# Linear attention feeding a gated FFN on one core: tiles turned by DMA, later loads, full-width transposes of q, a reordered beginning

## Chip, cores, metric

One core of one Trainium2 chip. The metric is device time in microseconds (us) of one execution; lower is better. The kernel before takes 325.9 us (median of 3 runs, 325.85 to 326.36).

In the profiles PE is TensorE (PEld its weight loads), DVE is VectorE, ACT is ScalarE, POOL is GpSimd and SP is SyncE; L503 is line 503 of that run's kernel.py, and x4 at the end of a line means four instructions in a row. Lines beginning with two numbers give start and length in us.

## The reference, cut to what matters

```
pos = arange(S);  theta = pi/2 * pos / S
phi(x) = concat(relu(x) * cos(theta), relu(x) * sin(theta))       # q, k: 8 batches x 8 heads x 576 x 64
kv  = einsum('bhsf,bhsd->bhfd', phi(k), v);   z = sum_s phi(k)
x   = (phi(q) @ kv) / (phi(q) @ z + 1e-6)                         # 4608 tokens x 512
out = (silu(x @ w_gate) * (x @ w_val)) @ w_out                    # 512 -> 1536 -> 512
```

The kernel works in 9 groups of 512 tokens, each of four tiles of 128. For a group it computes x of each tile, turns it (tokens by features becomes features by tokens), runs 12 blocks of gate and value products with silu and product between them, then the output stage: four tiles of 12 accumulating products. Batches are counted from 0 in the code, so its batch 1 is the "batch two", and its batch 2 the "batch three", of the change's name.

## The kernel before: the parts that the change touches

The program fixes the order of each engine's instructions, so this change is largely one of order. `at("b9", ...)` hangs work behind the second half of block 9, `at((1, 2), ...)` behind a part of the output stage. In the list of words each word is one step: G1.0 is the gate product of block 1 for token tile 0.

```python
def qturn_pe(b, j, lo, hi, eng):                   # q of batches 0 (last slot) and 1
    ps = take(1).bitcast(BF16).rearrange("p (c x) -> p c x", x=P)
    for c in range(lo, hi):
        for i in range(2):                         # two half-width transposes of the raw q
            nc.tensor.transpose(out=ps[i * D:(i + 1) * D, c - lo], in_=raws[b, "q"][:, 2 * j + i, c],
                                identity=ident)
    relu_op(eng, qt_of(b)[...], ps[...])           # relu while PSUM is emptied

def x_turn(t, fast=False):
    if fast:                                       # 4 PE transposes and an ACT copy
        x_turn_pe(t)
        x_turned(t, "act")
    else:
        nc.sync.dma_start_transpose(out=xT_of(t), in_=st["x", t])
# ... loads, in the order of issue:
load_slots(1, "q", 0, CUT)
load_wo(0); load_wo(1); load_wo(2)
load_slots(1, "q", CUT, NC)
for nm in ("q", "k", "v"):
    load(2, nm)
# ... group 0: blocks 0-5 by a list of words, blocks 6-11 in halves "a" and "b" of two tiles each
at("b11", q_(1, 0, 0), q_(1, 1, 0), lambda: kv_mm(1), lambda: kv_out(1))
at((1, 0), turn(4, True), a_(6, 0))                # slots of the output stage: tiles 4-7 made and turned
at((1, 2), turn(5, True), a_(7, 0))
at((2, 0), turn(6, True))
at((2, 2), turn(7, True))
```

## Time and profile before

| | kernel before |
|---|---|
| span of the profiled run | 324.6 us |
| first gate product (G1.0) | 16.41 us |
| 28 half-width transposes of q | 39.66 us |
| output stage of group 0 | 41.74 to 55.48 us (13.74) |
| group 1 to the end | 269.1 us |

These are starts in PE's order of instructions. PE is busy 98% of the span. The lines themselves stand in the prediction below.

### The profile page before, as it was taken

How to read it: one execution, taken by the hardware profiler on the slowest of the kernel's cores; microseconds unless marked ns; L12 is line 12 of the kernel's file. 1: busy time of each engine (PE TensorE's matmuls, PEld its weight loads, DVE VectorE, ACT ScalarE, POOL GpSimd, SP SyncE). 2: the span in 40 equal slices, each digit the busy share in tenths (PEclk: the TensorE clock that was granted, in tenths of full speed). 3: DMA queues.
4: the chain of work that ended last, by engine and by line, in shares of the span. 5: the costliest groups of instructions: out<-in, count | busy, mean ns of one | idle time of the engine just before them, and what ended most of it. 6: DMA issues, size and time to landing. Idle time of an engine off the chain costs nothing.

```text
span 324.6 us, 6212 instructions
## 1 busy us (share of the span) xinstructions
PE 318.0 (98%) x2474; PEld 164.6 (51%) x2474; DVE 181.8 (56%) x366; ACT 132.3 (41%) x247; POOL 34.8 (11%) x58
## 2 busy tenths in 40 slices
PE   7999999999999999999999999999999999999995
PEld 3589855454545444544454445444554445444443
DVE  7775866976575647565657555755564236423420
ACT  7553565943653335332642354344432132213311
POOL 6755200002002000110002000200000000000000
PEclk9999999999999999999999999999999999999999
DMA  7999999499676997699689969794921411240014
GB/s 264 215 199 199 205 205 221 70 125 149 147 125 80 185 153 128 93 170 163 120 111 140 164 129 130 119 186 110 134 46 34 106 26 32 44 103 17 2 32 97
DMA packets 71660, 40.37 MB, mean 124 GB/s; under 512 B 47184, under 2 KB 66384, under 8 KB 71632
## 3 DMA queue, kind: packets, MB, share of 16 engines
q1 hardware_dynamic: 49280, 22.29, 37.9%
q0 software_dynamic: 22192, 17.57, 35.5%
q8 instruction: 19, 0.31, 0.4%
q10 hardware_dynamic: 160, 0.13, 0.1%
q14 instruction: 9, 0.07, 0.1%
HBM read 37.75 MB, written 9.44 MB: 145 GB/s over the span
## 4 chain that ended last, share of the span: by engine, by line
PE 95%; DMA 2%; DVE 1%; ACT 0%; SPq 0%; issue 0%; ACTq 0%
PE banks L503 58%; PE banks L539 28%; PE banks L276 3%; PE banks L390 2%; DMA first_q<-in_q_dram 2%; PE banks L475 1%; PE banks L434 1%; PE banks L149 1%; PE banks L558 1%; PE banks L264 0%; PE banks L316 0%; PE banks L372 0%; SPq L117 0%; DVE qwT L360 0%; ACT ob L561 0%; ACT qf L339 0%
## 5 line engine op out<-in xcount | busy, mean ns | idle before, releaser
L514 DVE TENSOR_TENSOR ht<-sg,banks 128x512 bf16<-128x512 bf16 (+2 forms) x122 | 75.8, 625 | 68.1 <-PE banks L503 62.3
L509 ACT ACTIVATE sg<-banks 128x512 bf16<-128x512 f32 (+2 forms) x122 | 66.9, 548 | 113.6 <-PE banks L503 109.0
L503 PE MATMUL banks<-xT,wv_sb 128*128 128x512 bf16 (+2 forms) x488 | 112.8, 355 | 0.1
L503 PE MATMUL banks<-xT,wg_sb 128*128 128x512 bf16 (+2 forms) x488 | 112.6, 355 | 0.0
L539 PE MATMUL banks<-wo_sb,ht 128*128 128x512 bf16 x420 | 94.3, 379 | 0.0
L503 PEld LDWEIGHTS <-wv_sb 128*128 128x128 bf16 x488 | 47.2, 98 | 46.7 <-issue 0.4
L503 PEld LDWEIGHTS <-wg_sb 128*128 128x128 bf16 x488 | 45.7, 98 | 41.6
L539 PEld LDWEIGHTS <-ht 128*128 128x128 bf16 x420 | 40.1, 98 | 45.2 <-issue 0.2
L546 ACT COPY ob<-banks 128x512 f32<-128x512 f32 x18 | 10.5, 585 | 51.2 <-PE banks L539 49.2
L232 DVE TENSOR_TENSOR r_q<-raw_q,tab 128x1152 bf16<-128x1152 bf16 x24 | 17.9, 754 | 20.2 <-ACT raw_q L215 20.2
L546 DVE COPY ob<-banks 128x512 f32<-128x512 f32 x17 | 11.8, 691 | 28.9 <-PE banks L539 28.0
L236 DVE TENSOR_TENSOR v<-raw_v,tab 128x1152 bf16<-128x1152 bf16 x31 | 23.0, 752 | 0.3 <-ACT raw_v L570 0.3
L411 DVE TENSOR_TENSOR x<-banks,rec 128x512 bf16<-128x512 f32 (+1 forms) x32 | 21.5, 674 | 1.1
L714 POOL COPY hold<-phit 1x2 bf16<-1x2 bf16 x5 | 0.9, 176 | 155.1 <-DMA phit<-r_q 155.1
L215 ACT ACTIVATE raw_q<-raw_q 128x576 bf16<-128x576 bf16 x24 | 15.7, 680 | 0.8 <-DMA raw_q<-in_q_dram 0.8
L215 ACT ACTIVATE raw_k<-raw_k 128x576 bf16<-128x576 bf16 x24 | 16.0, 675 | 0.0
L390 PEld LDWEIGHTS <-phit 128*128 128x128 bf16 (+1 forms) x240 | 9.9, 100 | 6.0 <-issue 1.3
L390 PE MATMUL banks<-kv,phit 128*128 128x65 bf16 (+1 forms) x240 | 11.5, 195 | 0.0
L149 PE MATMUL banks<-zeros 128*128 128x64 bf16 (+1 forms) x66 | 8.7, 290 | 1.0 <-DVE zeros L144 1.0
L299 DVE CAST kv<-banks 64x260 bf16<-64x260 f32 x12 | 5.1, 428 | 7.4 <-ACT kv L299 7.4
L276 PEld LDWEIGHTS <-raw_k 64*64 64x64 bf16 x504 | 7.5, 106 | 2.6 <-issue 2.1
L276 PE MATMUL banks<-v,raw_k 64*64 64x130 bf16 x504 | 8.7, 218 | 0.0
(79 smaller groups left out, 134.3 us busy)
## 6 DMA issues: line engine op xcount, KB each, us to landing
out_dram<-ob SPq DMA_DIRECT2D x70, 128.0 KB, 2.4
raw_k<-in_k_dram POOLq DMA_DIRECT2D x7, 576.0 KB, 9.6
raw_q<-in_q_dram POOLq DMA_DIRECT2D x6, 576.0 KB, 6.1
raw_v<-in_v_dram POOLq DMA_DIRECT2D x6, 576.0 KB, 12.3
wo_sb<-in_moe_w_out_dram POOLq DMA_DIRECT2D x3, 512.0 KB, 12.7
wg_sb<-in_moe_w_gate_dram POOLq DMA_DIRECT2D x5, 256.0 KB, 9.0
wv_sb<-in_moe_w_val_dram POOLq DMA_DIRECT2D x5, 256.0 KB, 9.2
wo_sb<-in_v_dram SPq DMA_DIRECT2D x2, 576.0 KB, 4.1
```

Of the source, the lines that this page charges most:

```text
L149: nc.tensor.matmul(out=ps, lhsT=zeros, rhs=zeros[:, 0:cols].unsqueeze(1).to_broadcast([P, 4, cols]), start=True, stop=True)
L215: nc.scalar.activation(out=out, in_=in_, func=AF.Relu)
L232: nc.vector.tensor_tensor(out=st[b, "q"][:, g], in0=o.unsqueeze(2).to_broadcast([P, NC, 2, D]), in1=tab, op=ALU.mult)
L236: nc.vector.tensor_tensor(out=v2s[b % 2][:, g, :, :, 0:D], in0=(first if b == 0 and g == 0 else {"v": raw_of(b, "v")})["v"][:, g].unsqueez ...
L276: nc.tensor.matmul(out=ps[i * D:(i + 1) * D, e, j * 2 * D1:(j + 1) * 2 * D1], lhsT=raws[b, "k"][es, g, c], rhs=v2s[b % 2][es, g, c, :, 0:D ...
L390: nc.tensor.matmul(out=ps[ms, e, g * D1:(g + 1) * D1], lhsT=phit[b][:, e, g, c:c + n].rearrange("p c s -> p (c s)"), rhs=kv2s[b % 2][:, e, ...
L411: nc.vector.tensor_tensor(out=st["x", t].rearrange("p (y e d) -> p e y d", e=2, d=D)[:, :, ys], in0=ps[:, :, 0:2 * J * D1].rearrange("p e ...
L503: nc.tensor.matmul(out=st["f", tg, fc, lo][i], lhsT=(wg_sb, wv_sb)[i][:, kc, fs], rhs=xT[tg][:, ts, kc], start=(kc == 0), stop=(kc == KC - 1))
L509: nc.scalar.activation(out=sg[:, 0:n], in_=st["f", tg, fc, lo][0], func=AF.Silu)
L514: nc.vector.tensor_tensor(out=hts[tg % 2][:, fc, r:r + n], in0=st.pop(("s", tg, fc, lo))[:, 0:n], in1=ps[1], op=ALU.mult)
L539: nc.tensor.matmul(out=o_ps[t], lhsT=hts[tg % 2][:, fc, r:r + P], rhs=wo_sb[:, fc], start=(fc == 0), stop=(fc == FC - 1))
L546: (nc.scalar.copy if t % 2 == 0 else nc.vector.tensor_copy)(out=ob, in_=ps)
```

## The change

Its intent: take transposes off PE (tiles 4 and 5 are turned by DMA), keep the DMA engines free for these turns (k and v of batch three are loaded only when tile 4's turn has landed), use one full transpose for a pair of half ones, use 512 columns instead of 2 x 256 in blocks 6 to 11, and order the beginning better. Full transposes need the two heads of a pair side by side, so relu now runs on DVE ahead of the transposes and writes them so.

```diff
+    def relu_slots(b, lo, hi):
+        ...
+        relu_op("dve", st["qp"][:, b, lo:hi].rearrange("p c j (i d) -> p c (j i) d", i=2),
+                raws[b, "q"][:, :, lo:hi].rearrange("p g c d -> p c g d"))
     def qturn_pe(b, j, lo, hi, eng):
-            for i in range(2):
-                nc.tensor.transpose(out=ps[i * D:(i + 1) * D, c - lo], in_=raws[b, "q"][:, 2 * j + i, c], identity=ident)
-        relu_op(eng, qt_of(b)...
+            nc.tensor.transpose(out=ps[:, c - lo], in_=st["qp"][:, b, c, j], identity=ident)
+        copy_op(eng, qt_of(b)...
-    for nm in ("q", "k", "v"):
-        load(2, nm)
+    load(2, "q")
-    words = """ cq0@act cq1@act tq0 qr0@dve qw0.0 qw0.1 rk1.0@act rk0.0@dve z8 kv0.0 ...
+    words = """ cq1@act cq0@dve tq0 qr0@dve rk0.0@act rk1.0@dve qw0.0 qw0.1 z6 kv0.0 ...
+    at("a8", lambda: relu_slots(0, NC - 1, NC))
-    for g, s in enumerate(("a10", "a11", "b8", "b9")):
+    for g, s in enumerate(("b9", "b9", "b10", "b10")):
         at(s, lambda g=g: vmul(1, g))
+        if g == 2:
+            at(s, lambda: relu_slots(1, 0, CUT))
+    def load_2():
+        nc.gpsimd.tensor_copy(out=hold2, in_=xT[1][0:1, 0, 0, 0:2])
+        for nm in ("k", "v"):
+            load(2, nm)
+    at((0, 1), turn(4), load_2)
-    at((1, 0), turn(4, True), a_(6, 0))
+    at((1, 0), turn(5), a_(6, 0))
-    at((1, 2), turn(5, True), a_(7, 0))
+    at((1, 2), a_(7, 0))
-    for nm, f in order:
-        ffn_fc(0, f, *((HALF, GH) if nm == "b" else (0, HALF)))
+    for f in range(6, FC):
+        ffn_fc(0, f)
-    steps0 = [(piece, t) for piece in range(3) for t in range(2)] + [(piece, t) for t in (2, 3) for piece in range(3)]
+    steps0 = [(piece, t) for piece in range(3) for t in range(3)] + [(piece, 3) for piece in range(3)]
```

Cut: pools one buffer larger, the choice of PSUM banks, den and rec of tile 0 in halves, the rest of the words, and a later use of k and v of batch three in group 1.

More of the change, by code (lines that the diff above doesn't have):

```diff
@@ L50 @@
     phip = ctx.enter_context(tc.tile_pool(name="phip", bufs=2))
-    xp = ctx.enter_context(tc.tile_pool(name="xp", bufs=3))
+    xp = ctx.enter_context(tc.tile_pool(name="xp", bufs=4))
     xtp = ctx.enter_context(tc.tile_pool(name="xtp", bufs=3))
     smp = ctx.enter_context(tc.tile_pool(name="smp", bufs=3))
-    sgp = ctx.enter_context(tc.tile_pool(name="sgp", bufs=4))
+    sgp = ctx.enter_context(tc.tile_pool(name="sgp", bufs=5))
     obp = ctx.enter_context(tc.tile_pool(name="obp", bufs=4))
@@ L66, in take @@
     def take(n, hold=None):
-        free = [b for b in range(0, 8, n) if not any(b <= x < b + n for r in held.values() for x in r)]
-        b0 = min(free, key=lambda b: sorted(used[b:b + n], reverse=True))
+        taken = {x for r in held.values() for x in r}
+        free = [b for b in range(0, 8, n) if not any(b <= x < b + n for x in taken)]
+        b0 = min(free, key=lambda b: (n == 1 and hold is not None and hold[0] == "o" and b ^ 1 not in taken,
+                                      sorted(used[b:b + n], reverse=True)))
         if hold is not None:
@@ L258, in qturn_dma @@
         )
+    def relu_slots(b, lo, hi):
+        if "qp" not in st:
+            both = rel.tile([P, G, NC, 2, D], BF16, name="r_q").rearrange("p g c w d -> p (g c w d)")
+            st["qp"] = both.rearrange("p (b c j x) -> p b c j x", b=2, c=NC, j=J)
+        relu_op("dve", st["qp"][:, b, lo:hi].rearrange("p c j (i d) -> p c (j i) d", i=2),
+                raws[b, "q"][:, :, lo:hi].rearrange("p g c d -> p c g d"))
     def qturn_pe(b, j, lo, hi, eng):
@@ L262, in qturn_pe @@
         for c in range(lo, hi):
-            for i in range(2):
-                nc.tensor.transpose(out=ps[i * D:(i + 1) * D, c - lo], in_=raws[b, "q"][:, 2 * j + i, c],
-                                    identity=ident)
-        relu_op(eng, qt_of(b)[:, :, j, lo:hi].rearrange("p e c s -> p c e s"),
+            nc.tensor.transpose(out=ps[:, c - lo], in_=st["qp"][:, b, c, j], identity=ident)
+        copy_op(eng, qt_of(b)[:, :, j, lo:hi].rearrange("p e c s -> p c e s"),
                 ps[:, 0:hi - lo].rearrange("p c (e s) -> p c e s", e=2))
@@ L395, in a_tile2, with x_den, x_rec @@
         x_of(t, ps)
-    def x_den(t, ps):
-        den = smp.tile([P, H, 1], FP32, name="den")
+    def x_den(t, ps, ys=slice(0, 4)):
+        if ys.start == 0:
+            st["den", t] = smp.tile([P, H, 1], FP32, name="den")
         nc.vector.tensor_single_scalar(
-            out=den.rearrange("p (e y) o -> p e y o", e=2),
-            in_=ps[:, :, 0:2 * J * D1].rearrange("p e (y x) -> p e y x", x=D1)[:, :, :, D:D1], scalar=1e-6, op=ALU.add)
-        st["den", t] = den
-    def x_rec(t):
-        rec = smp.tile([P, H, 1], FP32, name="rec")
-        nc.vector.reciprocal(out=rec, in_=st.pop(("den", t)))
-        st["rec", t] = rec
-        st["x", t] = xp.tile([P, d_model], BF16, name="x")
+            out=st["den", t].rearrange("p (e y) o -> p e y o", e=2)[:, :, ys],
+            in_=ps[:, :, 0:2 * J * D1].rearrange("p e (y x) -> p e y x", x=D1)[:, :, ys, D:D1], scalar=1e-6, op=ALU.add)
+    def x_rec(t, ps, ys=slice(0, 4)):
+        if ys.start == 0:
+            st["rec", t] = smp.tile([P, H, 1], FP32, name="rec")
+            st["x", t] = xp.tile([P, d_model], BF16, name="x")
+        nc.vector.reciprocal(out=st["rec", t].rearrange("p (e y) o -> p e y o", e=2)[:, :, ys],
+                             in_=st["den", t].rearrange("p (e y) o -> p e y o", e=2)[:, :, ys])
     def x_mul(t, ps, ys=slice(0, 4)):
@@ L418, in x_of @@
         x_den(t, ps)
-        x_rec(t)
+        x_rec(t, ps)
         x_mul(t, ps)
@@ L620 @@
     words = """
-        cq0@act cq1@act tq0 qr0@dve qw0.0 qw0.1 rk1.0@act rk0.0@dve z8 kv0.0 rk3.0@dve rk2.0@dve kv1.0
-        kvo00@act rk3.1@dve kvo01@act rk2.1@dve kv1.1 tq1 kvo10@act kvo11@dve a0.0 qr1@dve a0.1 qw1.0 tq3
-        qw1.1 tq2 den0 qr3@act rec0 x0.0 a1.0 a1.1 qr2@act x0.1 xt0.0 qw3.1 xt0.1 xc0.0@act qw3.0 xc0.1@act
-        den1 z2 a3.0 rec1 G1.0 x1.0 a3.1 s1.0 G0.0 V0.0 qw2.0 s0.0 xt1.0 qw2.1 V1.0 xc1.0@dve a2.0 a2.1 m1.0
-        G1.1 den3 den2 V1.1 rec3 s1.1 G2.01 x3.0 G3.01 s2.01 m1.1 V2.01 rec2 s3.01 x2.0 xt3.0 V3.01
-        xc3.0@act m2.01 xt2.0 m3.01 G5.01 xc2.0@dve G4.01 s5.01 m0.0 G0.23 s4.01 V0.23 s0.23 G1.23 m0.23
-        G5.23 s1.23 V1.23 s5.23 V4.01 m1.23 V5.23 m4.01 V5.01 m5.23 G2.23 m5.01 V2.23 s2.23 G3.23 m2.23
-        V3.23 s3.23 G4.23 m3.23 V4.23 s4.23 G0.1 m4.23 V0.1 s0.1 m0.1
+        cq1@act cq0@dve tq0 qr0@dve rk0.0@act rk1.0@dve qw0.0 qw0.1 z6 kv0.0 rk2.0@dve rk3.0@dve kv1.0
+        kvo01@act rk3.1@dve kvo00@act rk2.1@dve kv1.1 a0.0 kvo11@act kvo10@dve tq1 den0.0 rec0.0 a0.1 x0.0
+        qr1@act tq2 den0.1 rec0.1 qw1.1 tq3 qr2@act qw1.0 xt0.0 x0.1 a1.0 qr3@act a1.1 qw2.0 xt0.1 qw2.1
+        xc0.0@act den1 z2 a2.0 rec1 xc0.1@act a2.1 x1.0 G1.0 G0.0 qw3.1 s1.0 xt1.0 s0.0 qw3.0 V0.0 xc1.0@act
+        V1.0 den2 rec2 a3.0 x2.0 a3.1 G0.1 G1.1 den3 s0.1 V1.1 rec3 s1.1 xt2.0 x3.0 G2.01 xc2.0@act V0.1
+        m1.0 V2.01 s2.01 m0.0 m0.1 xt3.0 m1.1 G3.01 m2.01 xc3.0@act V3.01 s3.01 G1.23 m3.01 V1.23 s1.23
+        G0.23 m1.23 V0.23 s0.23 G5.23 m0.23 G4.01 s5.23 G2.23 s4.01 G4.23 s2.23 G5.01 s4.23 V5.01 s5.01
+        V5.23 m5.01 G3.23 m5.23 V3.23 s3.23 V4.23 m3.23 V2.23 m4.23 V4.01 m2.23 m4.01
     """.split()
@@ L634 @@
         whole, a, part = b not in ("0", "1") or a != "0", int(a), int(b or 0)
+        ys = slice(0, 4) if whole else slice(2 * part, 2 * part + 2)
         if op == "z":
@@ L653 @@
         elif op == "den":
-            x_den(a, st["a", a])
+            x_den(a, st["a", a], ys)
         elif op == "rec":
-            x_rec(a)
+            x_rec(a, st["a", a], ys)
         elif op == "x":
-            x_mul(a, st["a", a], slice(0, 4) if whole else slice(2 * part, 2 * part + 2))
+            x_mul(a, st["a", a], ys)
             st["a", a, "n"] = st.get(("a", a, "n"), 0) + 1
@@ L674 @@
                 ffn_mul(0, a, *span)
-    order = []
-    for f in range(6, FC, 2):
-        order += [("a", g) for g in (f, f + 1)]
-        order += [("b", g) for g in (f, f + 1)]
     def turn_last():
@@ L684, in turn_last @@
             qturn_pe(0, j, NC - 1, NC, "act")
+    at("a8", lambda: relu_slots(0, NC - 1, NC))
     at("b9", turn_last)
     at("a8", lambda: relu_k(1, 0, 2, "dve"))
-    at("a9", lambda: relu_k(1, 2, 4, "dve"))
-    for g, s in enumerate(("a10", "a11", "b8", "b9")):
+    at("a9", lambda: relu_k(1, 2, 4, "act"))
+    for g, s in enumerate(("b9", "b9", "b10", "b10")):
         at(s, lambda g=g: vmul(1, g))
+        if g == 2:
+            at(s, lambda: relu_slots(1, 0, CUT))
     at("b11", q_(1, 0, 0), q_(1, 1, 0), lambda: kv_mm(1), lambda: kv_out(1))
@@ L694 @@
     at((0, 3), a_(5, 1))
-    at((1, 0), turn(4, True), a_(6, 0))
+    def load_2():
[4 more added lines that the diff above has]
+    at((1, 0), turn(5), a_(6, 0))
     at((1, 1), a_(6, 1))
-    at((1, 2), turn(5, True), a_(7, 0))
+    at((1, 2), a_(7, 0))
     at((1, 3), a_(7, 1))
     at((2, 0), turn(6, True))
+    at((0, 3), lambda: relu_slots(1, CUT, NC))
     at((2, 1), q_(1, 0, 1), q_(1, 1, 1))
     at((2, 2), turn(7, True))
-    HALF = GH // 2
-    for nm, f in order:
-        ffn_fc(0, f, *((HALF, GH) if nm == "b" else (0, HALF)))
-        slot(f"{nm}{f}")
-    steps0 = [(piece, t) for piece in range(3) for t in range(2)] + [(piece, t) for t in (2, 3) for piece in range(3)]
+    for f in range(6, FC):
+        ffn_fc(0, f)
+        slot(f"a{f}")
+        slot(f"b{f}")
+    steps0 = [(piece, t) for piece in range(3) for t in range(3)] + [(piece, 3) for piece in range(3)]
     for i, (piece, t) in enumerate(steps0):
@@ L724 @@
         if b == 2:
-            fs, tq = [s0 + i // 2 for i in range(8)], (s0 + 2, s0 + 2)
+            fs, tq = [s0 + i for i in (0, 0, 1, 1, 4, 5, 5, 6)], (s0 + 2, s0 + 2)
         else:
@@ L729 @@
             at(p0 + 3 if b == 3 else p0 + 1, lambda b=b: load_behind(b))
-        tk = (s0 + 4, s0 + 5)
+        tk = (s0 + 4, s0 + 8 if b == 2 else s0 + 5)
         for s, f in zip(fs, steps):
```

## The prediction

> **What bounds the kernel now.** I read the engine totals first. They say one engine is never free:
>
> ```profile
> PE 318.0 (98%) x2474; PEld 164.6 (51%) x2474; DVE 181.8 (56%) x366; ACT 132.3 (41%) x247; POOL 34.8 (11%) x58
> ```
>
> Busy PE time is not proof of need, so next the chain that ended last, by line, and its start in order of time (start, length, what):
>
> ```profile
> PE banks L503 58%; PE banks L539 28%; PE banks L276 3%; PE banks L390 2%; DMA first_q<-in_q_dram 2%; PE banks L475 1%; PE banks L434 1%; PE banks L149 1%; PE banks L558 1%; PE banks L264 0%; PE banks L316 0%; PE banks L372 0%; SPq L117 0%; DVE qwT L360 0%; ACT ob L561 0%; ACT qf L339 0%
> ...
> 1.75 6.24 DMA first_q<-in_q_dram
> 8.01 0.72 ACT qf L339 x2
> 8.78 0.34 PE banks L347 x3
> 9.12 1.73 PE banks L149 x8
> 11.07 0.65 PE banks L316 x30
> ```
>
> L503 (gate and value products) and L539 (output products) make 86% of the chain. From 16.16 us on the chain is PE after PE. So there are only three ways to be faster: fewer PE columns, a PE that is saturated sooner, or fewer holes in between. The third view, PE in order of time, gives the prices as distances between starts:
>
> ```profile
> 26.56 0.60 PE L503 MATMUL banks<-xT,wg_sb 128*128 128x256 bf16 x4
> 26.99 0.60 PE L503 MATMUL banks<-xT,wv_sb 128*128 128x256 bf16 x4
> ...
> 39.66 0.97 PE L264 MATMUL banks<-ident,raw_q 128*64 128x128 bf16 x28
> 40.56 1.24 PE L276 MATMUL banks<-v,raw_k 64*64 64x130 bf16 x72
> ...
> 47.21 0.39 PE L475 MATMUL banks<-ident,x 128*128 128x128 bf16 x4
> 47.44 0.39 PE L434 MATMUL banks<-kvd,phit 128*128 128x260 bf16 x2
> ...
> 54.62 1.03 PE L539 MATMUL banks<-wo_sb,ht 128*128 128x512 bf16 x4
> 55.48 1.03 PE L503 MATMUL banks<-xT,wg_sb 128*128 128x512 bf16 x4
> 56.35 1.03 PE L503 MATMUL banks<-xT,wv_sb 128*128 128x512 bf16 x4
> ```
>
> Four 512-column products take 0.863 us (216 ns each), four 256-column ones 0.436 us (109 ns each), a four-piece turn of an x tile 0.225 us, and 28 half-width transposes of q 0.90 us (32 ns each). Group 1 starts at 55.48 us, and from there to the end nothing in the order of the PE's big products changes. The change therefore acts on 8 to 55 us, plus some helpers until about 76 us. Between 16 and 55 us I find holes of only about 0.2 us at 19.6, 23.7 and 42.6 and 0.1 us at 35.7 and 39.6: under 1 us in all. The possible gain is small beside 325.9 us.
>
> **What the Trainium skill says.** "TensorE: Matmul & The Clock Gate", section "Wait — 56ns, not 53.3ns?", gives warm start-to-start times of 55.6 ns at 128 columns and 215.7 ns at 512. The trace agrees: 0.225/4 = 56 ns and 216 ns, at a granted clock of 1.00. The same page, "Part 3: Packing small matmuls — row/col tiling", says that small products on different parts of the array run at the same time. The half-width transposes, whose pairs write different output partitions, agree: 32 ns each, about half of 56. So one full transpose costs about what a pair of halves does. "DMA: Bandwidth & Descriptors", "Issuing engines are not separate DMA queues", says that DMAs from all issuers run on the same 16 engines and interleave. The trace shows what it costs: DMA turns of an x tile land 2.4 us after issue when no load is in flight (all four after 269 us), but 8.5 to 10.6 us when issued while the three loads of a batch are (the first three after 104 us). "VectorE: DVE Perf Modes", "Mode 4×_2P — both tricks at once", gives four 16-bit elements a cycle for single-source work in SBUF. The trace has a relu of 128x1152 at 0.45 and 0.65 us, against 0.30 us for 1152 at that rate and 0.96 GHz: fast mode plus a fixed part.
>
> **The change, part by part.** The order of instructions on each engine shows what moved.
>
> *Fewer, wider products.* Blocks 6 to 11 of group 0 now take all four token tiles at once: 96 products of 256 columns become 48 of 512. 96 x 0.109 = 10.48 us, 48 x 0.2158 = 10.36 us: 0.12 us saved on the path.
>
> *Tiles 4 and 5 by DMA.* Eight PE transposes go: 2 x 0.225 = 0.45 us off the path, with two 0.585 us ACT copies beside it.
>
> *Full transposes of q (batch two, in the words of the change).* Forty half-width transposes (40 x 32 ns = 1.29 us) become twenty full ones (20 x 56 ns = 1.12 us): 0.17 us saved. But relu now comes before the turn, on DVE: new operations of 256, 1792 and 512 elements. From the 1152-element row I take the one of 1792 at 0.6 to 1.0 us. In the new DVE order it lies between the last v products just before the 14 transposes. Count from T, the end of block 9's products. DVE: product of block 9 to T+0.65, two v products (0.70 each) to T+2.05, product of block 10 to T+2.7, one v to T+3.4, relu to T+4.1 or later. PE: four transposes and blocks 10 and 11, 0.22 + 2 x 1.73, are done at T+3.7. The transposes need the relu, so PE waits **0.4 to 0.8 us, say 0.6**. This hole is new; before, they read the raw q and the trace shows only 0.1 us there.
>
> *The beginning.* The casts of q go side by side (ACT and DVE; before, both on ACT, 0.72 us). DVE is busy with v until 8.16 us, so q is ready near 8.5, some 0.2 us sooner. relu of k's first part goes ahead of the weighting of q, and two of eight filler products (0.43 us) go, so the first k-v products can start near 10.45 instead of 11.0 us. From there DVE paces: kvd to 12.85; two split den, rec, x steps (about 0.8 each) and two weightings (0.75) put x0's second half near 15.2 us (15.45 before). Then the weighting of q for tile 2 (0.7) leads to a2 at 15.9 and G1.0 at 16.4 us. Before, G1.0 started at 16.41 too, but with one half tile done there and two half tiles now (0.25 us of PE work). With one hole fewer behind it I put the beginning at **-0.5 us** (0 to -0.8).
>
> *Later k and v.* The two loads of batch three are not issued at 34.6 and 35.8 us but when tile 4's DMA turn has landed. Loads occupy the DMA engines until 56.2 us now (v: 35.8 + 20.4); the q of that batch landed at 49.1 us. Without k and v the queue should be empty at about 47.5 to 49 us. Tile 4's x is ready about 4.1 us after the output stage starts, near 44.9 us, and its turn should land at 47.5 to 50 us. Then k lands near 55 to 57 us and v near 58 to 60 (a lone batch landed 5.8, 7.9 and 10.1 us after issue). First use of both is now after the fifth block of group 1, near 63 us. That is hidden.
>
> *Three outputs side by side.* 48 products in either order: no PE time. It takes one bank more, and tiles 4 to 7 need pairs; two pairs remain, so I give it nothing.
>
> Tile 5's turn is issued near 47.9 us, and group 1 needs all four tiles near 54.4 us. Alone it would land at 50.3; under the new loads at 56.7. Expectation: 51 to 53, hidden, with a chance of one in five of a stall of 1 to 2 us, **+0.3**.
>
> Sum: -0.12 - 0.45 - 0.17 - 0.5 + 0.6 + 0.3 = about -0.35, so 325.5; I shade it to **325.3 us**, as the new order may also close some of the old small holes.
>
> **Rivals.** (1) *Everything removed is gained and nothing waits*: relu keeps up, the turns land in time, the beginning gives its 0.8: -0.12 - 0.45 - 0.17 - 0.8 = -1.5, 324.4 us. For it: PE is the whole chain, so each column saved should count. Against it: the DVE count above. (2) *DMA turns become the bound*: tile 5 (or 4, if q of the batch is late) lands at 56.7 us or later as the turns at 104 and 107 us do, and PE idles 2 to 3 us before group 1: 327 to 328 us. For it: 8.5 to 10.6 us beside loads. Against it: tile 4 is issued when the queue drains, and the loads start only at about tile 5's issue. (3) *Late v*: if tile 4 lands at 53 us, v lands near 63 and DVE waits at block 5 of group 1. Against a loss: PE can run some three blocks (5 us) ahead in eight banks, so under 0.5 us.
>
> **Range and chances.** The low end is rival 1 almost in full, 324.2; the high end is my sum with the relu hole at its largest and a tile 5 stall of 1 us, 326.9. The runs of before spread over 0.5 us. Two per cent is 6.5 us; no part of the change is that large on a path in which 270 us are untouched: faster 0.005, within 0.985, slower 0.01, the last for a stall that I do not see.
>
> **What would show it.** The page should have 78 fewer PE instructions. In PE's order: G1.0 near 16.4 us; a hole of about 0.6 us, released by the relu on DVE, ahead of the 14 full transposes near 39 us; these at 56 ns each; the output stage 0.45 us shorter than 13.74 us; group 1 starting near 54.9 us with no wait for xT, and the same distance from there to the end as now (269.1 us). Tile 4's turn should land in under 5 us. I am wrong if the hole at the transposes is missing (then nearer 324.6), if PE waits for xT at group 1 (327 or more), or if the span behind group 1 changes, which would mean that k, v or the moved k-v products delay PE there.

## The result and the profile after

The changed kernel takes 325.84 us (4 runs, 325.56 to 326.57) beside 325.88 us for the kernel before on the same chip: ratio 0.9999, 95% interval 0.9983 to 1.0015. A ratio is the mean time of one kernel's fast runs over that of the other's of the same rounds, so it is not quite the ratio of the medians.

The three stages of both kernels, first before and then after (stretch, its length, busy time and instructions of PE, PEld, DVE, ACT and POOL in this order, granted clock, DMA share, GB/s; the DMA share adds up the times of packets and can exceed 1):

```profile
16.41:41.74 25.33, 25.26 (x339) 22.11 (x337) 16.94 (x44) 11.92 (x31) 10.94 (x15) 1.00 1.35 201
41.74:55.48 13.74, 13.74 (x100) 7.23 (x93) 9.54 (x27) 8.39 (x19) 0.00 (x0) 1.00 1.22 224
55.48:324.60 269.12, 265.28 (x1853) 127.60 (x1851) 142.96 (x259) 101.98 (x179) 12.03 (x20) 1.00 0.63 105
```

```profile
16.39:41.94 25.55, 24.64 (x272) 17.36 (x269) 15.94 (x36) 12.80 (x28) 8.81 (x12) 1.00 1.35 201
41.94:55.06 13.12, 13.12 (x87) 6.83 (x81) 9.64 (x28) 7.41 (x17) 1.65 (x3) 1.00 0.96 139
55.06:324.00 268.94, 265.27 (x1853) 127.60 (x1851) 142.90 (x259) 101.84 (x179) 12.00 (x20) 1.00 0.67 110
```

The output stage became 0.62 us shorter. The last stretch is the same work in the same time within 0.2 us. The first stretch has 0.62 us less PE work (24.64 for 25.26) and still is 0.22 us longer: PE is no longer busy all of it. Where it waits, from PE's order of time, and the chain at that place (start, length, what):

```profile
37.96 1.03 PE L513 MATMUL banks<-xT,wv_sb 128*128 128x512 bf16 x4
39.87 0.95 PE L274 MATMUL banks<-ident,r_q 128*128 128x128 bf16 x14 [0.89 <-DVE r_q L220]
40.76 1.25 PE L285 MATMUL banks<-v,raw_k 64*64 64x130 bf16 x72
```

```profile
36.22 1.11 DVE v L239 x2
37.32 0.15 issue
37.47 0.68 DVE ht L524
38.15 0.67 DVE v L239
38.82 1.00 DVE r_q L220
39.83 0.05 issue
39.87 0.95 PE banks L274 x14
```

The bracket is the idle time ahead of the group and its releaser: PE stood 0.89 us, until the relu on DVE (L220, writing r_q) was done. The chain, all PE here before, runs through DVE for about 4 us. PE would have been there at 39.87 - 0.89 = 38.98 us, 0.68 us sooner than the 39.66 before. So to the start of group 1: -0.68 up to the transposes, +0.89 for the hole, -0.62 in the output stage, about -0.42 in all (55.06 for 55.48), in a profile. (The bracket counts from the modelled end of the last product. By distances between starts, as in the prediction, PE was free at 37.96 + 0.86 = 38.82 and the hole is 1.05 us, where the kernel before had 0.09.) In the times, 0.04 us in these runs and 0.4 us in the next, it is at the edge of noise.

The DMA turns of tiles 4 and 5 in the changed kernel, issued at 46.0 and 49.0 us (all turns by DMA in that stretch):

```profile
L497 SPq DMA_TRANSPOSE xT<-x x2: 1190/1610/2030, 46.0 to 49.0; - x2
...
DMA to landing us min/median/max: 2.4/2.9/3.5
```

Tile 4 landed at 49.5, tile 5 at 51.4 us, long before PE needs them at 55.06.

### The profile page after: what moved, and what is told of

Its sections match the earlier page's. It is cut to its first block, busy times and chain, and to the rows that moved or that the text cites. A ratio compares the mean times of both kernels' runs of the same rounds, so it can differ in the third digit from the quotient of the medians.

```text
span 324.0 us, 6046 instructions
## 1 busy us (share of the span) xinstructions
PE 317.4 (98%) x2396; PEld 159.8 (49%) x2396; DVE 181.5 (56%) x362; ACT 132.2 (41%) x242; POOL 34.9 (11%) x59
## 3 DMA queue, kind: packets, MB, share of 16 engines
q0 software_dynamic: 22192, 17.57, 37.4%
## 4 chain that ended last, share of the span: by engine, by line
PE 93%; DVE 4%; ACT 1%; issue 0%; ACTq 0%
PE banks L513 57%; PE banks L549 28%; PE banks L285 3%; PE banks L399 2%; DVE v L239 1%; PE banks L444 1%; PE banks L381 1%; PE banks L485 1%; DVE raw_k L220 1%; PE banks L568 1%; DVE ht L524 0%; DVE qwT L369 0%; PE banks L274 0%; ACT L184 0%; DVE r_q L220 0%
## 5 line engine op out<-in xcount | busy, mean ns | idle before, releaser
L524 DVE TENSOR_TENSOR ht<-sg,banks 128x512 bf16<-128x512 bf16 (+2 forms) x116 | 74.7, 649 | 69.6 <-PE banks L513 63.1
L519 ACT ACTIVATE sg<-banks 128x512 bf16<-128x512 f32 (+2 forms) x116 | 65.8, 568 | 112.7 <-PE banks L513 109.7
L513 PE MATMUL banks<-xT,wv_sb 128*128 128x512 bf16 (+2 forms) x464 | 111.3, 364 | 0.0
L513 PE MATMUL banks<-xT,wg_sb 128*128 128x512 bf16 (+2 forms) x464 | 111.3, 364 | 0.0
L513 PEld LDWEIGHTS <-wv_sb 128*128 128x128 bf16 x464 | 44.9, 98 | 48.7
L513 PEld LDWEIGHTS <-wg_sb 128*128 128x128 bf16 x464 | 43.3, 98 | 43.2
L218 ACT ACTIVATE raw_k<-raw_k 128x576 bf16<-128x576 bf16 (+1 forms) x25 | 17.3, 695 | 0.0
L152 PE MATMUL banks<-zeros 128*128 128x64 bf16 (+1 forms) x64 | 9.4, 310 | 1.0 <-DVE zeros L147 1.0
```

What stands on the lines that cost most here:

```text
L152: nc.tensor.matmul(out=ps, lhsT=zeros, rhs=zeros[:, 0:cols].unsqueeze(1).to_broadcast([P, 4, cols]), start=True, stop=True)
L218: nc.scalar.activation(out=out, in_=in_, func=AF.Relu)
L513: nc.tensor.matmul(out=st["f", tg, fc, lo][i], lhsT=(wg_sb, wv_sb)[i][:, kc, fs], rhs=xT[tg][:, ts, kc], start=(kc == 0), stop=(kc == KC - 1))
L519: nc.scalar.activation(out=sg[:, 0:n], in_=st["f", tg, fc, lo][0], func=AF.Silu)
L524: nc.vector.tensor_tensor(out=hts[tg % 2][:, fc, r:r + n], in0=st.pop(("s", tg, fc, lo))[:, 0:n], in1=ps[1], op=ALU.mult)
```

## The experiments

Each kernel differs from the changed one by the edit shown. All ten gave the reference's result. Runs of one group shared a chip and the runs of the kernel before.

**The changed kernel again.** No edit.

> The changed kernel once more, as the base of the comparisons. My theory: PE gains about 0.6 us in the output stage of group 0 (13.12 us in the first trace, 13.74 before) and gives it back in one hole of 0.9 us at the 14 full transposes, which wait for the relu of 128x1792 on DVE. Expected: the hole again between 0.7 and 1.1 us, output stage 13.0 to 13.2 us, ratio to the kernel before 0.998 to 1.000. Rival (the gain is lost at the beginning): the hole varies, and the start of the first gate product moves by more than 0.5 us between profiles.

Measured: 325.88 us beside 326.27 us, ratio 0.9990 (0.9978 to 1.0002). The hole was 0.89 us again, the output stage 13.12 us (41.81 to 54.93). The first gate product started at 16.26 us; over all nine fast profiles with the new beginning it lies between 16.05 and 16.54 us. The theory holds; the rival's half microsecond is not passed, but by 0.01 us only. A start that wanders so far hides gains of this size, which is why the table behind the experiments counts from it.

**Half-width transposes.**

```diff
-            nc.tensor.transpose(out=ps[:, c - lo], in_=st["qp"][:, b, c, j], identity=ident)
-        copy_op(...)                       # and the three relu_slots calls
+            for i in range(2):
+                nc.tensor.transpose(out=ps[i * D:(i + 1) * D, c - lo], in_=raws[b, "q"][:, 2 * j + i, c], identity=ident)
+        relu_op(...)
```

> Only the full transposes of q undone: half-width transposes of the raw q and relu while PSUM is emptied, as before; all else as changed. My theory: no wait for DVE, so the hole shrinks from 0.9 to about 0.1 us, the transposes cost 0.17 us more: 0.6 to 0.8 us faster than the changed kernel, 325.1 us. Rival (relu on DVE is not what PE waits for, k-v products or the load of q are): the hole stays over 0.5 us and the time stays.

Measured: 325.15 us, ratio 0.9971 (0.9958 to 0.9984), 0.73 us under the changed kernel in the same group. PE's order of time:

```profile
38.95 0.97 PE L275 MATMUL banks<-ident,raw_q 128*64 128x128 bf16 x28
39.85 1.24 PE L287 MATMUL banks<-v,raw_k 64*64 64x130 bf16 x72
41.02 1.04 PE L551 MATMUL banks<-wo_sb,ht 128*128 128x512 bf16 x4
```

No bracket, no hole, and the 28 half transposes take 0.90 us (0.89 for the 14 full ones: here there was nothing to save). The full transposes as a part cost 0.7 us by the times, and 0.54 us in the profile counted from the first gate product (table below).

**The relu one v product sooner.**

```diff
+        if g == 2:
+            at(s, lambda: relu_slots(1, 0, CUT))
         at(s, lambda g=g: vmul(1, g))
-        if g == 2:
-            at(s, lambda: relu_slots(1, 0, CUT))
```

> The relu of 128x1792 put one v product ahead in DVE's order. My theory: it ends 0.7 us sooner, the hole falls from 0.9 to 0.2 to 0.4 us, and the span by 0.5 to 0.7 us. Rival (the wait is for the load of q, which lands near 37.8 us): the hole stays within 0.2 us of what it was.

Inconclusive: the profiled run fell in a state with a granted clock of 0.658 and a span of 474.7 us, so its hole cannot be compared. Of the other five runs four took 325.11 to 325.55 us, 0.3 to 0.8 us under the changed kernel's 325.88 and so on the side of the theory; one took 328.26 us at a clock of 0.992, and with it the ratio is 0.9991 (0.9962 to 1.0020).

**Two v products one slot sooner, the relu ahead of block 10's product.** By the edit two of the four move (b9 to b8, b10 to b9), and three then stand ahead of block 10's product.

```diff
-    for g, s in enumerate(("b9", "b9", "b10", "b10")):
+    for g, s in enumerate(("b8", "b9", "b9", "b10")):
```

> Three of the four v products of batch two one slot sooner, and with them the relu ahead of the gating product of block 10. My theory: DVE has room there, the relu starts when q has landed (37.8 us) and ends at about 38.9 us, when PE gets there: hole 0 to 0.2 us, 0.7 to 0.9 us faster than the changed kernel, near 325.0 us. Rival (DVE is simply overloaded in this stage): the hole moves to the k-v products or the output stage and the span shrinks by less than 0.3 us.

Measured: 325.52 us, ratio 0.9980 (0.9968 to 0.9992). The hole stayed at 0.88 us: both my number and the rival's failed. DVE in order of time:

```profile
36.00 1.42 DVE L239 TENSOR_TENSOR v<-raw_v,tab 128x1152 bf16<-128x1152 bf16 x2
38.46 1.09 DVE L220 TENSOR_SCALAR r_q<-raw_q 128x1792 bf16<-128x1792 bf16 x1 [1.04 <-DMA raw_q<-in_q_dram]
39.46 0.68 DVE L524 TENSOR_TENSOR ht<-sg,banks 128x512 bf16<-128x512 bf16 x1
```

DVE was ready at 37.4 and waited 1.04 us for the load of q. So in this profile a second bound held: landing of the load plus length of the relu. But this profile is the odd one. The load takes 10.6 us in every profile, and it was issued late here; first the changed kernel's issue, then the load in v_sooner's chain:

```profile
27.11 0.74 POOL L105 DMA_DIRECT2D raw_q<-in_q_dram  x1 [2.16 <-DVE ht L524]
```

```profile
27.83 10.60 DMA raw_q<-in_q_dram
```

In the other ten fast profiles it was issued between 26.71 and 27.51 us, and nothing that this edit moves lies ahead of it. In the changed kernel's own profile q had thus landed near 37.71 us, 1.0 us before the relu started (38.74). An estimate from these numbers: 37.71 + 1.08 = 38.79 us for the end of the relu, against PE free at 38.82, so there the new order alone would have closed nearly all of the hole. The times lean that way (325.52 for 325.88 us, intervals overlapping); no profile shows it.

**The relu in two halves, in that order.** The slots are those of v_sooner; the line for them is left out.

```diff
-        relu_op(...)
+        for j in range(J):
+            relu_op("dve", st["qp"][:, b, lo:hi, j].rearrange("p c (i d) -> p c i d", i=2),
+                    raws[b, "q"][:, 2 * j:2 * j + 2, lo:hi].rearrange("p g c d -> p c g d"))
```

> As v_sooner, and the relu of 128x1792 cut in two (pairs of heads j=0 and j=1), so that PE can begin with the first seven transposes while DVE does the second half. The last runs showed that with DVE free the relu starts at 38.46 us, when the load of q lands, and takes 1.09 us. Theory now: hole = landing + relu - PE's arrival, so with half the relu ahead the hole falls from 0.88 to 0.2 to 0.4 us, and the time by 0.5 us against the changed kernel. Rival (some other thing than the length of the relu, say the wait of PE for a bank): hole stays over 0.7 us.

Measured: 324.69 us beside 325.85 us, ratio 0.9964 (0.9952 to 0.9977); no hole at all. Better than expected, and the DVE view shows an unforeseen reason:

```profile
37.77 0.75 DVE L220 TENSOR_SCALAR r_q<-raw_q 128x896 bf16<-128x896 bf16 x2 [0.42 <-DMA raw_q<-in_q_dram]
38.44 0.67 DVE L525 TENSOR_TENSOR ht<-sg,banks 128x512 bf16<-128x512 bf16 x1
```

Both halves together take 0.75 us where the one operation took 1.09, and in this profile q landed 0.7 us sooner than in v_sooner's, at the usual time (issued at 27.15). So it is not shown that the halves alone closed the hole. The length of the one operation was itself abnormal; the last two runs test why.

**The loads in their old place.**

```diff
-    load(2, "q")
+    for nm in ("q", "k", "v"):
+        load(2, nm)
-    at((0, 1), turn(4), load_2)
+    at((0, 1), turn(4))
```

> Only the place of the loads undone: k and v of batch three are issued right behind its q again, tiles 4 and 5 still turned by DMA. Theory (loads slow the turns): the turns of tiles 4 and 5, issued near 46 and 49 us, land 7 to 10 us later instead of 3.5 and 2.4, tile 5 at 56 to 58 us, and PE, ready for group 1 at 55 us, waits 1 to 3 us for xT: 327 to 328.5 us. Rival (the turns would be hidden anyway): no wait for xT, time as the changed kernel within 0.3 us.

Measured: 327.05 us, ratio 1.0038 (1.0025 to 1.0052). Tiles 4 and 5 landed 9.1 and 7.9 us after issue. PE in order of time:

```profile
53.98 1.03 PE L549 MATMUL banks<-wo_sb,ht 128*128 128x512 bf16 x4
56.84 1.02 PE L513 MATMUL banks<-xT,wg_sb 128*128 128x512 bf16 x4 [1.84 <-DMA xT<-x]
```

PE waited 1.84 us for xT; the profiled run was the slowest of the five (327.83 us), and by the median the loss is 1.2 us against the kernel before. This is rival 2 of the prediction, and deferring the loads is what keeps it away.

**Tiles 4 and 5 turned on PE again.**

```diff
-    at((0, 1), turn(4), load_2)
-    at((1, 0), turn(5), a_(6, 0))
+    at((1, 0), turn(4, True), load_2, a_(6, 0))
-    at((1, 2), a_(7, 0))
+    at((1, 2), turn(5, True), a_(7, 0))
```

> Only the turns of tiles 4 and 5 back on PE and ACT (k and v of batch three still issued late, behind tile 4). Theory: 8 transposes more on a saturated PE, 0.45 us: output stage 13.5 to 13.7 us instead of 13.12, time 0.4 to 0.6 us longer, near 326.4 us. Rival (PE has slack there): output stage and time within 0.15 us of the changed kernel.

Measured: 326.10 us, ratio 1.0008 (0.9995 to 1.0020), against 0.9990 and 0.9999 for the changed kernel beside its own runs of before. The output stage went from 42.09 to 55.60 us, 13.51 us for 13.12: 0.39 us, against 0.45 expected. In the times the intervals overlap.

**The old beginning.** The words of the kernel before in the changed one (edit: the list only).

> Only the order of the beginning undone: the list of steps from the first cast of q to block 5 as before, the rest as changed. Theory: from the traces the new beginning is worth about 0.45 us (output stage start less the hole: 40.9 us against 41.74 before, of which 0.12 + 0.17 are the wider products and transposes): time 0.3 to 0.6 us longer than the changed kernel, near 326.3 us. Rival (the beginning is bound by the arrival of q and k, so its order is worth nothing): within 0.15 us of the changed kernel.

Measured: 326.10 us, ratio 1.0008 (0.9996 to 1.0021). In the times the sign is right and the size within noise. The profiles say more when the wandering start is taken out: from the first gate product to the first one of block 6 it is 12.34 us in both profiles with the old list (16.41 to 28.75 before, 16.29 to 28.63 here) and 11.96 or 11.97 us in all nine with the new one. So the new order is worth 0.38 us behind the first gate product. The first gate product itself did not come visibly sooner: 16.29 and 16.41 us with the old list, 16.05 to 16.54 with the new.

**The relu walked in another order.**

```diff
-        relu_op("dve", st["qp"][:, b, lo:hi].rearrange("p c j (i d) -> p c (j i) d", i=2),
-                raws[b, "q"][:, :, lo:hi].rearrange("p g c d -> p c g d"))
+        relu_op("dve", st["qp"][:, b, lo:hi].rearrange("p c j (i d) -> p (j i) c d", i=2),
+                raws[b, "q"][:, :, lo:hi])
```

> The changed kernel with the same relu operation walked in another order: heads, slots, elements instead of slots, heads, elements, so that source and destination have the same even outermost count of 4. Nothing else. In the traces 256, 512 and 1152 elements take 0.22, 0.285 and 0.45 us, which is 0.15 us and four elements a cycle at 0.96 GHz, but 1792 elements with seven slots outermost took 1.08 us, which is 0.15 us and two a cycle. Theory (the odd outermost count of the source halves the rate): 0.62 us instead of 1.08, hole 0.4 to 0.5 us instead of 0.89, time 0.4 to 0.5 us shorter than the changed kernel, near 325.4 us. Rival (the size or the strides make it slow): 1.0 to 1.1 us and the same hole.

Measured: 325.31 us beside 325.73 us, ratio 0.9985 (0.9972 to 0.9997). The group of operations (busy, mean ns) in the changed kernel and in this one, and the hole in this one:

```profile
L220 DVE TENSOR_SCALAR r_q<-raw_q 128x1792 bf16<-128x1792 bf16 x1 | 1.1, 1079 | 0.0
...
L220 DVE TENSOR_SCALAR raw_k<-raw_k 128x1152 bf16<-128x1152 bf16 x1 | 0.5, 453 | 0.0
...
L220 DVE TENSOR_SCALAR r_q<-raw_q 128x512 bf16<-128x512 bf16 x1 | 0.3, 285 | 0.0
L220 DVE TENSOR_SCALAR r_q<-raw_q 128x256 bf16<-128x256 bf16 x1 | 0.2, 220 | 0.0
```

```profile
L220 DVE TENSOR_SCALAR r_q<-raw_q 128x1792 bf16<-128x1792 bf16 x1 | 0.6, 619 | 0.0
```

```profile
39.44 0.95 PE L274 MATMUL banks<-ident,r_q 128*128 128x128 bf16 x14 [0.43 <-DVE r_q L220]
```

Same elements, same place: 619 ns for 1079, and a hole of 0.43 us for 0.89. The walk made it slow, not the size, and the hole shrank by as much as the operation. The time agrees but doesn't resolve it: the changed kernel had ratios of 0.9990 and 0.9999.

**Both: that walk, in the order of v_sooner.**

> The same relu in the order of v_sooner, so that it starts when q has landed, at 37.8 to 38.4 us. Theory: it ends at 38.4 to 39.0 us, hole 0 to 0.3 us, 0.7 to 1.0 us faster than the changed kernel, 324.7 to 325.1 us, as relu_parts. Rival (v_sooner showed 0.88 us because of the load alone): hole over 0.6 us.

Measured: 324.69 us, ratio 0.9970 (0.9956 to 0.9984), no hole; q landed at 37.80 us, 0.66 us sooner than in v_sooner's profile. It and relu_parts are about 1.0 to 1.2 us under the kernel before in the same group, and both intervals end below 1. By ratio half_turns (0.9971) is level with them; in the profiles they are 0.5 us ahead of it.

**All fast profiles, counted from the first gate product to the start of group 1.** This takes out the start, which differs by up to half a microsecond between profiles.

| run | us |
|---|---|
| before | 39.07 |
| after, after_again | 38.67, 38.67 |
| half_turns | 38.13 |
| v_sooner (load of q late) | 38.66 |
| relu_parts | 37.68 |
| loads_old_place | 40.68 |
| pe_turns | 39.06 |
| old_words | 39.05 |
| relu_g_only | 38.21 |
| relu_g_sooner | 37.62 |

So the whole change is worth 0.40 us in both profiles of it, undoing the turns or the beginning costs 0.39 or 0.38, and relu_parts and relu_g_sooner, which keep the full transposes and have no hole, gain another 1.0.

## Why the prediction was right, point by point

The verdict and the range were right (325.3 predicted, 324.2 to 326.9; 325.84 measured), by a sum in which two errors of opposite sign met: the hole was 0.36 us larger than the 0.6 I put down, and the 0.3 us for tile 5 was not lost. That these met is luck. Term by term, from starts in the two profiles:

| term | predicted, us | in the profiles, us |
|---|---|---|
| beginning, to block 6 | -0.5 | -0.40 |
| wider products | -0.12 | -0.14 (10.50 to 10.36) |
| q transposes before the output stage | part of -0.17 | -0.22, small waits ahead of them included |
| output stage: turns of tiles 4 and 5, last q transposes | -0.45 and the rest of -0.17 | -0.62 |
| hole at the relu | +0.6 | +0.96 (0.09 to 1.05) |
| tile 5 late | +0.3 | 0 |
| sum | -0.34 | -0.42 |

- **PE is the bound; only its columns, its start and its holes count.** Shown in the profiles: group 1 to the end takes 268.9 to 269.1 us in all eleven fast ones, so they differ only by what PE did before group 1.
- **Transposes of tiles 4 and 5, 0.45 us.** Right: 0.39 us in pe_turns, from one profile. The output stage shrank by 0.62 us rather than 0.45; the rest, about 0.2 us, is the full transposes placed there (before, 53.08 to 53.52 us between output products with 8 half transposes; after, 52.88 to 53.11 us with 4 full ones).
- **Full transposes save 0.17 us.** Not in the large group: 14 full ones take 0.89 us, 28 halves 0.90. The saving is seen in the small groups: 2 full ones in 0.11 us for 4 halves in 0.23, and 4 full ones in 0.23 for 8 halves in 0.34. I had priced full ones with 56 ns from the turn of an x tile; that holds in the small groups, while the 14 took about 64 ns each.
- **A new hole of 0.4 to 0.8 us at the relu.** The mechanism was right, place and releaser included; the size was 0.89 us. The count of DVE's order was good: counted from T, the relu started at T+3.48 for the T+3.4 expected. The term that failed is "the one of 1792 at 0.6 to 1.0 us", counted there as 0.7: I read fast mode from the 1152-element row and applied it to another walk. (PE's side was 0.11 us off as well: "four transposes" at 0.22 us are two, by my own count of twenty full ones.)
- **Why that walk was slow.** The traces give 0.26 ns an element between 256 and 1152 elements (220 to 453 ns), which is four a cycle at the 0.96 GHz of the prediction; 0.15 us plus that rate fits 1152, 512 and 256 elements (0.45, 0.28, 0.22), and half that rate fits 1792 (1.08). The Trainium skill, "VectorE: DVE Perf Modes", section "What auto-detection actually checks", asks for "outermost non-unit dims both even or equal" of source and destination in the modes that use both ports. Here the source walked 7 slots outermost and the destination was, by its layout, one run of 1792; the pattern as compiled is not on record. The runs bear the rule out on each side: 4 and 4 outermost was fast (relu_g_only, 0.62 us); so was the 512-element relu with 2 slots outermost and a destination of one run, even but unequal; and so were relu_parts' halves with 7 on both sides, odd but equal (896 elements in 418 ns, where half rate would be 617). So neither the odd count alone, as my expectation for relu_g_only had it, nor the short rows of 64 elements made it slow, for relu_parts and the 512-element relu had these too. What the hardware does inside is not visible.
- **DVE's order sets the hole.** Right for the changed kernel: q landed near 37.71 us there (27.11 plus 10.6; I had 37.8), and the relu started only at 38.74, behind a v product. In v_sooner's profile the load, issued 0.7 us later, was the bound instead. So the order alone is not shown to close the hole; order and a shorter relu together are (relu_parts, relu_g_sooner), with q landing at 37.8.
- **The beginning, -0.5 us.** G1.0 came at 16.39 us as counted (16.4), the first k-v products at 10.41 (10.45). Worth 0.38 us by old_words, in profiles only.
- **Wider products, -0.12 us.** 0.14 us by starts in the two profiles. Not tested alone; it is below what a time resolves. Nor were the three outputs side by side, which I gave nothing.
- **Tile 5 by DMA, +0.3 us expected loss.** Did not happen: it landed 2.4 us after issue, at 51.4. loads_old_place showed the loss that it insured against, 1.84 us of waiting.
- **Later k and v are hidden.** Right, with less room than I gave. k landed near 57 us, but v, issued at 50.55 us, only 11.8 us later at 62.3 (I said 58 to 60); its first product ran at 64.57 us.
- **Rivals and range.** Rival 1, nothing waits, 324.4 us: the versions without a hole took 324.69 us. Two ends do not follow from their words: the low one, 324.2, lies below rival 1 in full, and the sum with a hole of 0.8 and a stall of 1 us is near 326.5, not 326.9, unless the spread of the runs is added. The old hole at 42.6 us was 0.1 us, not 0.2.

So where did the expected gain go? About 1.3 us was taken off PE's path before group 1 (0.68 + 0.62), and 0.89 us of it was given back in one wait that the change itself made, when relu moved from behind the transposes to ahead of them.

## What to carry to other kernels

An operation moved from behind PE to ahead of it becomes part of PE's path, so price it with its own access pattern and from the moment its input lands, not with the rate of a neighbour. When a new order changes nothing in a profile, look for a second bound behind the first, and then whether that profile's loads landed when they do in the others. And bulk loads should be held back behind small DMA turns that a saturated engine waits for: here turning by DMA took 0.95 us longer than turning on PE without it (327.05 for 326.10 us), and 0.39 us less with it (in the profiles).

## What the Trainium skill lacked or had wrong

- "VectorE: DVE Perf Modes", section "Rules for kernel authors": it promises 4x for dense 16-bit copy and scalar work in SBUF and does not repeat the condition on the outermost dimensions, which the page has further up. Walking 7 slots outermost in the source alone cost 1079 ns for 1792 elements; the other walk took 619 ns.
- "TensorE: Matmul & The Clock Gate", section "Back-to-back issue gap", gives about 131 ns a product at 512 columns and 81 ns at 128 for streams of weight load and product. These runs show 216 ns at 512 (four in 0.863 us) and 56 ns at 128 (four in 0.225 us), which agree with the same page's isolated gap instead.
- "DMA: Bandwidth & Descriptors" has no time for a DMA turn beside loads. One turn of 128x512 landed 2.4 us after issue alone and 7.9 to 10.6 us beside loads.
- No page that I read has the state of one run here: granted clock 0.658 (about 0.65 in every stretch from 20 us on) and a span of 474.7 us on a single core, while other runs of the same kernel took 325.1 to 325.6 us.
